# Row sums folded on GpSimd and VectorE instead of TensorE, and float64 weights rebuilt by arithmetic instead of by moved bits, in an attention and feed-forward kernel on one Trainium2 core

## The chip, the cores and the metric

The kernel runs on one core of a Trainium2 chip. The metric is the device time of one execution in microseconds; lower is better. The engines are called PE (TensorE), DVE (VectorE), ACT (ScalarE), POOL (GpSimd) and SP (SyncE, which issues most of the DMAs). Each engine works through its own list of instructions in order, and waits on semaphores for what other engines make.

## The reference

```python
# attention: q, k, v of (8, 12, 448, 64) float32, gains g_q, g_k of 64
q_n, k_n = rmsnorm(q, g_q), rmsnorm(k, g_k)      # x / sqrt(mean(x*x) + 1e-6) * g
attn = softmax(q_n @ k_n.T / sqrt(64))
x = (attn @ v), heads joined                      # (3584, 768)
# feed-forward: w_in (768, 1024) and w_out (1024, 768) are float64, g_ln of 1024
h = x @ w_in
solu = h * softmax(h)
ln = (solu - mean) / sqrt(var + 1e-6) * g_ln
out = (ln @ w_out).astype(float32)                # (3584, 768)
```

The weights come in as float64 numbers, and the kernel makes float32 of them on the chip: it loads each number as two 32-bit words, `lo` and `hi`.

## The kernel before, in words

The function that does the work is `fast_path`. (`general_path`, for inputs outside a range, is behind a branch on a flag that is read at the very end; it does not run here.) Instructions are issued in an order written out by hand: the code runs a list of "units", and after each unit `unit` emits what `later(k, f)` put off for k units, and then one stage of the weight conversion in progress (`feed`).

**Attention.** 48 pairs (8 batches, 6 pairs of heads), index `n`. A pair is loaded four ahead (`load(n + 4)`, eight DMAs of q and k), squared on ACT three ahead (`squares`), and summed along each half row on DVE (`row_sums`, tile `part`, 128 x 28). A row of 64 lies as two halves of 32 in two groups of 32 partitions, so the two half sums must be added across partitions: `fold_sums(n + 2)` does it with a product by a constant matrix `fold` on PE, into a PSUM tile `ss`. From `ss`, `rsqrt_seed` (a logarithm and an exponential on ACT, and `nx` on DVE) and `rsqrt_step` (three small DVE operations) make the reciprocal root `ny`; `normalise` multiplies on POOL (`qkn`), `qk_transpose` transposes on DVE (`qkT`, called T in the prediction), `gain` scales on ACT. Then, for each of four key blocks `kc`: `scores(n, kc)` is two products on PE (`s`) and two exponentials on ACT (`E`); `add` sums the blocks of E for the softmax's denominator, the first on POOL, the other two on DVE (`es`). `values(n - 1)` (`o`) and `sums(n - 1)` (`sm`) on PE stand between the second and the third block of the pair, and `divide(n - 1)` on DVE ends with `xT`.

**PSUM.** The tiles `s`, `ss`, `o`, `sm`, `pu` and `po` share a pool of six buffers (tag "t"); a product waits until an earlier tile's readers have released its buffer. `h` has one buffer of its own.

**Weights.** 12 steps of 512 columns (w_in) during pairs 0 to 11, and 16 steps of 384 columns (w_out) during pairs 12 to 21. A step has four stages: two ACT passes that shift the low word by arithmetic (`low_bits`, lines 469 and 470), two DVE operations on the high word (`high_bits`, 473 and 474), one DVE operation that joins them (`join`, 478), and, for w_out, an ACT pass that multiplies by the gain (`product`, 483). This moving of bits is right only for numbers in a certain range.

**Feed-forward.** 28 tiles of 128 tokens. `ff_in` (`h`) starts in pair 13; `ff_max`, `ff_moments` and `ff_norm` work on DVE, ACT and POOL; `ff_transpose` (`pu`, `uT`) and `ff_out` (`po`, `y`) start in pair 23, when all of w_out is converted. What is left after the last pair is issued unit by unit.

**Check.** During those last units each weight chunk is loaded once more (`again`), `check_w` takes the smallest and largest magnitude of its high words on DVE, and `check_all` puts the result, by a small product on PE (`pw`, line 502), into the flag.

Of the kernel before, what the change touches and what calls it, by code (L numbers as in the profile page):

```python
# [9 lines left out]
FP32 = mybir.dt.float32  # L10
# [356 lines left out]
def fast_path(  # L367
# [7 lines left out]
    out: bass.AP,  # L375
    grow: bass.AP,
    within: bass.AP,
    large: bass.AP,
):


# [24 lines left out]

    ident = consts.tile([P, P], FP32, name="ident")
    ones = consts.tile([P, D], FP32, name="ones")
    fold = consts.tile([P, 2, 2, 32], FP32, name="fold")
    w_in = consts.tile([P, KD, DFF], FP32, name="w_in")  # L410
    w_out = consts.tile([P, KF, DM], FP32, name="w_out")
    gcol = consts.tile([P, KF + 2], FP32, name="gcol")
    mhalf = consts.tile([P, 1], FP32, name="mhalf")
    seven = consts.tile([P, 1], FP32, name="seven")
    eps = consts.tile([P, 1], FP32, name="eps")

    def setup():

        nc.scalar.add_instruction(
            mybir.InstLoadActFuncSet(  # L420
                act_func_set_id=6, name=nc.get_next_instruction_name(), engine=mybir.EngineType.Activation
            )
        )
        nc.gpsimd.memset(mhalf, -0.5)
        nc.gpsimd.memset(seven, 7.0)
        nc.gpsimd.memset(eps, 1e-6)
        nc.gpsimd.memset(ones, 1.0)
        make_identity(nc, ident)

        nc.gpsimd.memset(fold, 0.0)  # L430
        for g in range(4):
            gs = slice(g * 32, g * 32 + 32)
            for x in range(2):
                nc.gpsimd.tensor_copy(fold[gs, g // 2, x], ident[gs, gs])
        pg = ps_t.tile([P, KF + 2], FP32, tag="t", name="pg")
        nc.tensor.transpose(pg, grow, ident[0 : KF + 2, 0 : KF + 2])
        nc.vector.tensor_copy(gcol, pg)

        nc.vector.tensor_scalar(
            gcol[:, KF : KF + 1], gcol[:, KF : KF + 1], gcol[:, KF + 1 : KF + 2], within, OP.mult, OP.mult  # L440
        )

# [13 lines left out]
    def convert_w(step, raw):  # L460

        _, dst, c, cols = step
        n = cols.stop - cols.start
        lo, hi = raw[:, :, 0], raw[:, :, 1]
        tmp = work.tile([P, 2, n], U32, tag="uT", name="tmp")
        t, low = tmp[:, 0], tmp[:, 1].bitcast(FP32)

        def low_bits():
            nc.scalar.activation(low, lo, AF.Relu, scale=-(2.0 ** -29), bias=seven)  # L469
            nc.scalar.activation(tmp[:, 1].bitcast(I32), low, AF.Copy, scale=-1.0, bias=7.0)  # L470

        def high_bits():
            nc.vector.tensor_scalar(t, hi, 3, 0x3FFFFFFF, OP.logical_shift_left, OP.bitwise_and)
            nc.vector.scalar_tensor_tensor(t, hi, 0xC0000000, t, OP.bitwise_and, OP.bitwise_or)  # L474

        def join():
            o = dst[:, c, cols].bitcast(U32) if dst is w_in else t
            nc.vector.tensor_tensor(o, t, tmp[:, 1], OP.bitwise_or)

        def product():  # L480
            if dst is w_out:

                nc.scalar.activation(dst[:, c, cols], t.bitcast(FP32), AF.Copy, scale=gcol[:, c : c + 1])

        return [low_bits, high_bits, join, product]

    def check_w(x, raw):

        hi = raw[:, :, 1].bitcast(FP32)
        nc.vector.tensor_reduce(extent[:, 0, x : x + 1], hi, AX, OP.min, apply_absolute_value=True)  # L490
        nc.vector.tensor_reduce(extent[:, 1, x : x + 1], hi, AX, OP.max, apply_absolute_value=True)

    def check_all():


        worst = small.tile([P, 2], FP32, tag="mv", name="worst")
        one = small.tile([1, 2], FP32, tag="one", name="one")
        pw = ps_t.tile([1, 2, P], FP32, tag="t", name="pw")
        nc.vector.tensor_reduce(worst[:, 0:1], extent[:, 0], AX, OP.min)
        nc.vector.tensor_reduce(worst[:, 1:2], extent[:, 1], AX, OP.max)  # L500
        for i in range(2):
            nc.tensor.transpose(pw[:, i], worst[:, i : i + 1], ident)
        nc.vector.tensor_reduce(one[:, 0:1], pw[:, 0], AX, OP.min)
        nc.vector.tensor_reduce(one[:, 1:2], pw[:, 1], AX, OP.max)
        nc.vector.tensor_scalar(one[:, 0:1], one[:, 0:1], 2.0 ** -15, None, OP.is_ge)
        nc.vector.tensor_scalar(one[:, 1:2], one[:, 1:2], 122880.0, None, OP.is_lt)
        nc.vector.tensor_tensor(one[:, 0:1], one[:, 0:1], one[:, 1:2], OP.mult)

        nc.vector.tensor_scalar(one[:, 1:2], large, -1.0, 1.0, OP.mult, OP.add)
        nc.vector.tensor_tensor(one[:, 0:1], one[:, 0:1], one[:, 1:2], OP.mult)  # L510
        nc.vector.tensor_scalar(large, one[:, 0:1], -1.0, 1.0, OP.mult, OP.add)

    st = {}
    xTs = {}
# [29 lines left out]
    def row_sums(n):  # L544
        d = st[n]
        d["part"] = small.tile([P, 2 * NB], FP32, tag="part", name="part")
        nc.vector.tensor_reduce(d["part"], d["sq"], AX, OP.add)  # L547

    def fold_sums(n):
        d = st[n]  # L550
        d["ss"] = ps_t.tile([P, 2 * NB], FP32, tag="t", name="ss")
        nc.tensor.matmul(d["ss"], fold.rearrange("p h x t -> p (h x t)"), d["part"], start=True, stop=True)

    def rsqrt_seed(n):

# [174 lines left out]
    def unit(f):  # L730
        nonlocal now
        f()
        now += 1
        due = [x for x in todo if x[0] <= now]
        todo[:] = [x for x in todo if x[0] > now]
        for _, g in sorted(due, key=lambda x: x[0]):
            g()
        feed()
# [6 lines left out]
    W_OUT = 22  # L745
    raws = []
    stages = []
    extent = consts.tile([P, 2, len(wq)], FP32, name="extent")
    wdone = 0
    wtarget = 0  # L750

# [34 lines left out]
    def prepare(n):  # L786
        squares(n)
        row_sums(n)

    N = B * NP  # L790
    load(0)
# [7 lines left out]
    with tc.manual_schedule():  # L799
        prepare(0)  # L800
        wtarget = 1
        unit(lambda: fold_sums(0))
        rsqrt_seed(0)
        rsqrt_step(0)
        normalise(0)
        prepare(1)
        qk_transpose(0)
        gain(0)
        unit(lambda: fold_sums(1))
        load(3)  # L810
        rsqrt_seed(1)
        rsqrt_step(1)
# [5 lines left out]
        for n in range(N):  # L818
# [35 lines left out]
                unit(lambda: values(n - 1))  # L854
            if n + 3 < N:
                row_sums(n + 3)
            if n and n + 1 < N:
                load_v(n + 1)
            convert(4)
# [8 lines left out]
        unit(lambda: None)  # L868
        unit(lambda: values(N - 1))
        unit(lambda: sums(N - 1))  # L870

        last = events[at:]
        assert len(last) > len(wq) + 1
        again = [load_w(wq[x]) for x in range(2)]
        for x, (_, f) in enumerate(last):
            unit(f)
            if x < len(wq):
                check_w(x, again[x])
                if x + 2 < len(wq):
                    again.append(load_w(wq[x + 2]))  # L880
            if x == len(wq) + 1:
                check_all()
        for _ in range(4):
            unit(lambda: None)

# [1 line left out]
@with_exitstack  # L887
def kernel(
    ctx: ExitStack,
    tc: tile.TileContext,  # L890
    q: bass.AP,
    k: bass.AP,
    v: bass.AP,
    g_q: bass.AP,
    g_k: bass.AP,
    moe_w_in: bass.AP,
    moe_w_out: bass.AP,
    moe_g_ln: bass.AP,
    out: bass.AP,
):  # L900
    nc = tc.nc
    D = q.shape[3]
    P = 128
    KF = moe_w_in.shape[1] // P
    gains = ctx.enter_context(tc.tile_pool(name="gains", bufs=1))
    grow = gains.tile([KF + 2, P], FP32, name="grow")
    gg = gains.tile([P, 2, D], FP32, name="gg")
    gmax = gains.tile([P, 1], FP32, name="gmax")
    within = gains.tile([P, 1], FP32, name="within")
    flag = gains.tile([1, 1], I32, name="flag")  # L910
    large = gains.tile([1, 1], FP32, name="large")
    nc.scalar.dma_start(grow[0:KF, :], moe_g_ln.rearrange("(c p) -> c p", p=P))
    for i, g in enumerate((g_q, g_k)):
        for h in range(2):
            nc.scalar.dma_start(grow[KF + i : KF + i + 1, h * D : (h + 1) * D], g.rearrange("(o d) -> o d", o=1))
    for i, g in enumerate((g_q, g_k)):
        nc.scalar.dma_start(gg[:, i], g.rearrange("(o d) -> o d", o=1).to_broadcast([P, D]))

    nc.vector.tensor_tensor(gg[:, 0], gg[:, 0], gg[:, 1], OP.mult)
    nc.vector.tensor_reduce(gmax, gg[:, 0], AX, OP.max, apply_absolute_value=True)  # L920
    nc.vector.tensor_scalar(large, gmax[0:1], 80.0 / float(D) ** 0.5, None, OP.is_gt)
    nc.vector.tensor_scalar(within, gmax, 80.0 / float(D) ** 0.5, float(D) ** -0.5, OP.is_le, OP.mult)
    fast_path(tc, q, k, v, moe_w_in, moe_w_out, out, grow, within, large)
    nc.vector.tensor_copy(flag, large)
    other = nc.values_load(flag[0:1, 0:1], min_val=0, max_val=1)
    with tc.If(other > 0):
        general_path(tc, q, k, v, g_q, g_k, moe_w_in, moe_w_out, moe_g_ln, out)


# [28 lines left out]
```

## Time and profile before

| | us |
|---|---|
| median of 4 timed runs | 1127.38 (1127.1 to 1128.03) |
| the profiled execution, its own time | 1126.35 |
| its span in the profile | 1124.5 |
| PE busy | 1041.3 (93%) |
| DVE busy | 604.8 (54%) |
| ACT busy | 381.6 (34%) |
| POOL busy | 210.9 (19%) |

The busy share of an engine is a mean over stages with different limits. By windows of the same trace, PE is busy 625.60 of 625.60 us from 358.70 to 984.30, and 132.11 of 135.70 us from there to 1120; from 55 to 184 us it is busy 100.21 of 129.00 us, DVE 103.93, ACT 64.20 and POOL 41.41. PE's records overlap, so busy PE times of single groups add up to more than they cost. Profile lines show: start and length in us (timeline), or the count, busy time, mean ns of one and the idle time before them with what ended it (groups). In a line, "L552" is line 552 of the kernel before.

### The profile page before, as it was taken

The page shows a single profiled execution, that of the slowest core. Times are in us where ns is not written, and L with a number is a line of the kernel's source. Part 1 is how long each engine was busy: PE and PEld are TensorE (multiplying, and loading weights), DVE is VectorE, ACT ScalarE, POOL GpSimd, SP SyncE. Part 2 cuts the span into 40 slices and gives each one's busy share as a digit, 9 for nine tenths or more (in the row PEclk, how much of TensorE's full clock was granted, in tenths as well). Part 3 has the DMA queues.
Part 4 walks back from the last instruction along what each step waited for, and adds up shares of the span by engine and source line. Part 5 has one row for each costly group of instructions (what it writes and reads, how often), then busy time and mean ns, then how long its engine had stood idle before and what let it go on. Part 6 is the DMA issues. An engine that isn't in the chain of part 4 may idle for free.

```text
span 1124.5 us, 10697 instructions
## 1 busy us (share of the span) xinstructions
PE 1041.3 (93%) x3619; PEld 479.9 (43%) x3619; DVE 604.8 (54%) x1013; ACT 381.6 (34%) x789; POOL 210.9 (19%) x143
## 2 busy tenths in 40 slices
PE   2878788798889999999999999999999999999997
PEld 1323232233334444444444444444444444455554
DVE  3688787455788544444444444444445544555521
ACT  2744554224756222222222222232224322311110
POOL 2432223011333111111111111121111211100000
PEclk9998988999889999999999999999999999999999
DMA  6544334103544111111111111131111201033341
GB/s 129 117 96 98 88 84 98 22 23 67 116 106 75 39 39 39 39 39 38 39 39 33 32 38 39 39 64 30 39 33 33 54 23 59 15 127 117 100 142 42
DMA packets 234426, 70.10 MB, mean 62 GB/s; under 512 B 223600, under 2 KB 223608, under 8 KB 234360
## 3 DMA queue, kind: packets, MB, share of 16 engines
q1 hardware_dynamic: 230016, 58.23, 24.0%
q10 hardware_dynamic: 4344, 11.08, 2.5%
q8 instruction: 31, 0.51, 0.2%
q14 instruction: 35, 0.29, 0.1%
HBM read 58.27 MB, written 11.01 MB: 62 GB/s over the span
## 4 chain that ended last, share of the span: by engine, by line
PE 73%; DVE 13%; ACT 6%; issue 3%; DMA 2%; SPq 2%; POOL 1%; ACTq 0%; DVEq 0%; POOLq 0%
PE h L658 26%; PE po L709 26%; PE s L595 8%; PE o L618 8%; DVE es L609 4%; PE pu L699 2%; PE sm L627 2%; SPq L528 2%; DVE qkT L582 1%; DVE part L547 1%; DVE tmp L474 1%; ACT E L599 1%; ACT qkT L586 1%; DVE r L642 1%; ACT tmp L469 1%
## 5 line engine op out<-in xcount | busy, mean ns | idle before, releaser
L658 PE MATMUL h<-w_in,xT 128*128 128x512 f32 x672 | 308.0, 609 | 11.7 <-DVE u L676 11.7
L709 PE MATMUL po<-w_out,uT 128*128 128x384 f32 x896 | 297.9, 489 | 2.1 <-ACT uT L700 2.1
L709 PEld LDWEIGHTS po<-w_out,uT 128*128 128x128 f32 x896 | 168.3, 190 | 132.0 <-issue 15.0
L595 PE MATMUL s<-qkT 64*112 64x448 f32 x768 | 200.8, 581 | 19.0 <-DVE nx L560 8.4
L599 ACT ACTIVATE E<-s 112x448 f32<-112x448 f32 x384 | 177.3, 546 | 103.9 <-PE s L595 103.8
L658 PEld LDWEIGHTS h<-w_in,xT 128*128 128x128 f32 x672 | 127.3, 194 | 169.4 <-issue 164.7
L618 PE MATMUL o<-E,v 112*64 112x448 f32 x768 | 169.8, 588 | 12.4 <-DVE xT L644 12.4
L607 POOL TENSOR_TENSOR es<-E 112x896 f32<-112x896 f32 x48 | 104.0, 2166 | 325.6 <-ACT E L599 325.6
L595 PEld LDWEIGHTS s<-qkT 64*112 64x112 f32 x768 | 78.2, 176 | 133.7 <-issue 69.0
L609 DVE TENSOR_TENSOR es<-es,E 112x896 f32<-112x896 f32 x96 | 125.0, 1302 | 13.7 <-ACT E L599 10.5
L572 POOL TENSOR_TENSOR qkn<-qk,ny 128x896 f32<-128x896 f32 x48 | 82.8, 1724 | 146.7 <-DVE ny L567 122.8
L700 DVE COPY uT<-pu 128x512 f32<-128x512 f32 x28 | 19.3, 688 | 160.1 <-PE pu L699 144.0
L671 ACT ACTIVATE u<-h,hmax 128x1024 f32<-128x1024 f32 x28 | 31.2, 1115 | 210.6 <-DVE hmax L668 210.6
L710 ACT COPY y<-po 128x384 f32<-128x384 f32 x56 | 26.9, 480 | 213.6 <-PE po L709 213.6
L618 PEld LDWEIGHTS o<-E,v 112*64 112x64 f32 x768 | 54.5, 146 | 102.0 <-issue 83.4
L686 POOL TENSOR_TENSOR he<-he,mhalf 128x1 f32<-128x1 f32 x28 | 21.8, 778 | 382.6 <-DVE he L685 382.6
L668 DVE TENSOR_REDUCE hmax<-h 128x1 f32<-128x1024 f32 x28 | 34.3, 1224 | 80.4 <-PE h L658 80.4
L560 DVE TENSOR_SCALAR nx<-ss 128x28 f32<-128x28 f32 x48 | 9.0, 188 | 115.2 <-ACT ny L559 115.2
L586 ACT ACTIVATE qkT<-qkT,gcol 128x448 f32<-128x448 f32 x48 | 32.6, 680 | 75.6 <-DVE qkT L582 75.6
L640 DVE STREAM_TRANSPOSE r<-sm 128x448 f32<-128x448 f32 x48 | 31.0, 646 | 47.0 <-PE sm L627 47.0
L542 ACT ACTIVATE sq<-qk 128x896 f32<-128x896 f32 x48 | 45.7, 952 | 28.9 <-ACT y L710 11.3
L547 DVE TENSOR_REDUCE part<-sq 128x28 f32<-128x896 f32 x48 | 51.8, 1078 | 6.5 <-ACT sq L542 6.5
(67 smaller groups left out, 610.9 us busy)
## 6 DMA issues: line engine op xcount, KB each, us to landing
raw<-in_moe_w_in_dram SPq DMA_DIRECT2D x24, 512.0 KB, 3.7
raw<-in_moe_w_out_dram SPq DMA_DIRECT2D x32, 384.0 KB, 3.3
qk<-in_q_dram SPq DMA_DIRECT2D x192, 56.0 KB, 2.3
qk<-in_k_dram SPq DMA_DIRECT2D x192, 56.0 KB, 2.3
v<-in_v_dram SPq DMA_DIRECT2D x48, 224.0 KB, 3.0
out_dram<-y ACTq DMA_DIRECT2D x28, 384.0 KB, 2.3
grow<-in_g_q_dram ACTq DMA_DIRECT2D x2, 0.2 KB
grow<-in_g_k_dram ACTq DMA_DIRECT2D x2, 0.2 KB
```

What stands on the lines that cost most here:

```text
L542: nc.scalar.activation(d["sq"], d["qk"].rearrange("p s b d -> p (s b) d"), AF.Square)
L547: nc.vector.tensor_reduce(d["part"], d["sq"], AX, OP.add)
L572: nc.gpsimd.tensor_tensor(d["qkn"], d["qk"].rearrange("p s b d -> p (s b) d"), d["y"].rearrange("p b -> p b ()").to_broadcast([P, 2 * NB, ...
L586: nc.scalar.activation(d["qkT"][:, 0], d["qkT"][:, 0], AF.Copy, scale=gcol[:, KF : KF + 1])
L595: nc.tensor.matmul(s, d["qkT"][hh, 1, kc * SP : (kc + 1) * SP], d["qkT"][hh, 0, :], start=True, stop=True)
L599: nc.scalar.activation(d["E"][:, kc, h], d["s", h], AF.Exp)
L607: nc.gpsimd.tensor_tensor(d["es"], d["E"][:, 0], d["E"][:, 1], OP.add)
L609: nc.vector.tensor_tensor(d["es"], d["es"], d["E"][:, kc], OP.add)
L618: nc.tensor.matmul(d["o"][h * D : (h + 1) * D, :], d["v"][:, h, kc], d["E"][:, kc, h], start=(kc == 0), stop=(kc == NJ - 1),)
L658: nc.tensor.matmul(d["h"][:, hs], xTs[m][:, c, i * P : (i + 1) * P], w_in[:, c, hs], start=(c == 0), stop=(c == KD - 1))
L668: nc.vector.tensor_reduce(nmax, d["h"], AX, OP.max, negate=True)
L709: nc.tensor.matmul(po, d["uT"][:, c], w_out[:, c, hs], start=(c == 0), stop=(c == KF - 1))
```

## The change

Three things change together.

1. *Fold.* `swap_sums` copies the half sums, four groups of 32 partitions, to the neighbouring group on POOL, into an SBUF tile `ss`; it is put off by three units after `row_sums(n + 3)`, so it stands in POOL's list behind the `qkn` of pair n + 2 and before the `es` of pair n + 1, one pair ahead of its use. `fold_sums` then is one DVE addition, between the qkT transpose and `nx`. The `fold` matrix and its product on PE are gone; `ss` no longer takes a PSUM buffer, and `nx` reads SBUF.
2. *Conversion.* Mantissa and exponent are taken apart, made into numbers, and multiplied: `fields` (two DVE operations), `scale` (two ACT passes), `join` (three DVE operations), and `product`, on POOL for w_in and on DVE for w_out. It is right for the whole range of float32.
3. *Check.* The second load of the weights, `check_w` and `check_all` are gone; the flag is written once, at the start.

```diff
-    fold = consts.tile([P, 2, 2, 32], FP32, name="fold")
...
-        t, low = tmp[:, 0], tmp[:, 1].bitcast(FP32)
-        def low_bits():
-            nc.scalar.activation(low, lo, AF.Relu, scale=-(2.0 ** -29), bias=seven)
-            nc.scalar.activation(tmp[:, 1].bitcast(I32), low, AF.Copy, scale=-1.0, bias=7.0)
-        def high_bits():
-            nc.vector.tensor_scalar(t, hi, 3, 0x3FFFFFFF, OP.logical_shift_left, OP.bitwise_and)
-            nc.vector.scalar_tensor_tensor(t, hi, 0xC0000000, t, OP.bitwise_and, OP.bitwise_or)
+        e, m = tmp[:, 0], tmp[:, 1].bitcast(FP32)
+        ei = e.bitcast(I32)
+        def fields():
+            nc.vector.tensor_scalar(tmp[:, 1], hi, 0xFFFFF, None, OP.bitwise_and)
+            nc.vector.tensor_scalar(e, hi, 20, 0x7FF, OP.logical_shift_right, OP.bitwise_and)
+        def scale():
+            nc.scalar.activation(m, tmp[:, 1], AF.Copy, scale=2.0 ** -20, bias=1.0)
+            nc.scalar.activation(ei, ei, AF.Relu, bias=m896)
         def join():
-            o = dst[:, c, cols].bitcast(U32) if dst is w_in else t
-            nc.vector.tensor_tensor(o, t, tmp[:, 1], OP.bitwise_or)
+            nc.vector.scalar_tensor_tensor(m, lo, 2.0 ** -52, m, OP.mult, OP.add)
+            nc.vector.tensor_scalar(ei, ei, 255.0, 2.0 ** 23, OP.min, OP.mult)
+            nc.vector.scalar_tensor_tensor(e, hi, 0x80000000, e, OP.bitwise_and, OP.bitwise_or)
         def product():
-            if dst is w_out:
-                nc.scalar.activation(dst[:, c, cols], t.bitcast(FP32), AF.Copy, scale=gcol[:, c : c + 1])
+            if dst is w_in:
+                nc.gpsimd.tensor_tensor(dst[:, c, cols], m, e.bitcast(FP32), OP.mult)
+            else:
+                nc.vector.scalar_tensor_tensor(
+                    dst[:, c, cols], m, gcol[:, c : c + 1], e.bitcast(FP32), OP.mult, OP.mult
+                )
...
+    def swap_sums(n):
+        d = st[n]
+        d["ss"] = small.tile([P, 2 * NB], FP32, tag="ss", name="ss")
+        for g in range(4):
+            o = g ^ 1
+            nc.gpsimd.tensor_copy(d["ss"][g * 32 : g * 32 + 32], d["part"][o * 32 : o * 32 + 32])
     def fold_sums(n):
         d = st[n]
-        d["ss"] = ps_t.tile([P, 2 * NB], FP32, tag="t", name="ss")
-        nc.tensor.matmul(d["ss"], fold.rearrange("p h x t -> p (h x t)"), d["part"], start=True, stop=True)
+        nc.vector.tensor_tensor(d["ss"], d["ss"], d["part"], OP.add)
...
     def prepare(n):
         squares(n)
         row_sums(n)
+        swap_sums(n)
...
             if n + 3 < N:
                 row_sums(n + 3)
+                later(3, lambda n=n: swap_sums(n + 3))
...
-        again = [load_w(wq[x]) for x in range(2)]
-        for x, (_, f) in enumerate(last):
+        for _, f in events[at:]:
             unit(f)
-            if x < len(wq):
-                check_w(x, again[x])
-                if x + 2 < len(wq):
-                    again.append(load_w(wq[x + 2]))
-            if x == len(wq) + 1:
-                check_all()
```

More of the change, by code (lines that the diff above doesn't have):

```diff
@@ L377, in fast_path @@
     within: bass.AP,
-    large: bass.AP,
 ):
@@ L413, in fast_path @@
     mhalf = consts.tile([P, 1], FP32, name="mhalf")
-    seven = consts.tile([P, 1], FP32, name="seven")
+    m896 = consts.tile([P, 1], FP32, name="m896")
     eps = consts.tile([P, 1], FP32, name="eps")
@@ L424, in setup @@
         nc.gpsimd.memset(mhalf, -0.5)
-        nc.gpsimd.memset(seven, 7.0)
+        nc.gpsimd.memset(m896, -896.0)
         nc.gpsimd.memset(eps, 1e-6)
@@ L428, in setup @@
         make_identity(nc, ident)
[L430 to L434, printed above, removed]
         pg = ps_t.tile([P, KF + 2], FP32, tag="t", name="pg")
@@ L480, in product @@
         def product():
-            if dst is w_out:
-                nc.scalar.activation(dst[:, c, cols], t.bitcast(FP32), AF.Copy, scale=gcol[:, c : c + 1])
[L485 to L511, printed above, removed]
@@ L513, in fast_path @@
+            if dst is w_in:
[4 more added lines that the diff above has]
+                )
+        return [fields, scale, join, product]
     st = {}
@@ L747, in fast_path @@
     stages = []
-    extent = consts.tile([P, 2, len(wq)], FP32, name="extent")
     wdone = 0
@@ L801, in fast_path @@
         wtarget = 1
-        unit(lambda: fold_sums(0))
+        fold_sums(0)
         rsqrt_seed(0)
@@ L808, in fast_path @@
         gain(0)
-        unit(lambda: fold_sums(1))
+        fold_sums(1)
+        unit(lambda: None)
         load(3)
@@ L870, in fast_path @@
         unit(lambda: sums(N - 1))
-        last = events[at:]
-        assert len(last) > len(wq) + 1
-        again = [load_w(wq[x]) for x in range(2)]
-        for x, (_, f) in enumerate(last):
+        for _, f in events[at:]:
             unit(f)
-            if x < len(wq):
-                check_w(x, again[x])
-                if x + 2 < len(wq):
-                    again.append(load_w(wq[x + 2]))
-            if x == len(wq) + 1:
-                check_all()
         for _ in range(4):
@@ L910 @@
     flag = gains.tile([1, 1], I32, name="flag")
-    large = gains.tile([1, 1], FP32, name="large")
     nc.scalar.dma_start(grow[0:KF, :], moe_g_ln.rearrange("(c p) -> c p", p=P))
@@ L920 @@
     nc.vector.tensor_reduce(gmax, gg[:, 0], AX, OP.max, apply_absolute_value=True)
-    nc.vector.tensor_scalar(large, gmax[0:1], 80.0 / float(D) ** 0.5, None, OP.is_gt)
+    nc.vector.tensor_scalar(flag, gmax[0:1], 80.0 / float(D) ** 0.5, None, OP.is_gt)
     nc.vector.tensor_scalar(within, gmax, 80.0 / float(D) ** 0.5, float(D) ** -0.5, OP.is_le, OP.mult)
[L923 to L926, printed above, removed]
+    fast_path(tc, q, k, v, moe_w_in, moe_w_out, out, grow, within)
+    large = nc.values_load(flag[0:1, 0:1], min_val=0, max_val=1)
+    with tc.If(large > 0):
         general_path(tc, q, k, v, g_q, g_k, moe_w_in, moe_w_out, moe_g_ln, out)
```

## The prediction

> **What bounds the kernel now.** First the page's slices: where is TensorE (PE) full, and where is it not?
>
> ```profile
> PE   2878788798889999999999999999999999999997
> DVE  3688787455788544444444444444445544555521
> PEclk9998988999889999999999999999999999999999
> ```
>
> Each digit is 28.1 us. From slice 14 on PE is full; asked by windows, it is busy 625.60 of the 625.60 us from 358.7 to 984.3. Before 358.7 us it is not, and VectorE (DVE) is at 7 to 8 tenths. So the span has two regimes: 358.7 us of attention pairs with the weight conversion beside them, and 766 us in which only PE time counts. Next, the groups that the change touches:
>
> ```profile
> L552 PE MATMUL ss<-part,fold 128*128 128x28 f32 x96 | 21.0, 300 | 21.3 <-DVE part L547 14.5 <-DVE r L640 3.8 <-ACT E L599 3.0
> L560 DVE TENSOR_SCALAR nx<-ss 128x28 f32<-128x28 f32 x48 | 9.0, 188 | 115.2 <-ACT ny L559 115.2
> L609 DVE TENSOR_TENSOR es<-es,E 112x896 f32<-112x896 f32 x96 | 125.0, 1302 | 13.7 <-ACT E L599 10.5
> ```
>
> Columns: busy us, mean ns, idle before and its releaser. Seen: DVE stands 115.2 us at L560 behind ScalarE (ACT), and 1302 ns is a mean over adds of 1.08 us and stretched ones. The timeline of one w_in pair shows both; pairs repeat every 12.88 us (qkT transpose T at 123.81 and 136.70):
>
> ```profile
> 132.17 2.46 POOL L607 TENSOR_TENSOR es<-E 112x896 f32<-112x896 f32 x1 [0.43 <-ACT E L599]
> 132.61 4.18 DVE L609 TENSOR_TENSOR es<-es,E 112x896 f32<-112x896 f32 x2
> 136.70 1.10 DVE L582 STREAM_TRANSPOSE qkT<-qkn 128x896 f32<-128x896 f32 x1
> 137.84 0.67 ACT L586 ACTIVATE qkT<-qkT,gcol 128x448 f32<-128x448 f32 x1 [5.74 <-DVE qkT L582]
> 138.41 0.75 ACT L469 ACTIVATE tmp<-raw,seven 128x512 f32<-128x512 uint32 x1
> 139.19 0.63 ACT L470 ACTIVATE tmp<-tmp 128x512 int32<-128x512 f32 x1
> 139.73 0.27 ACT L559 ACTIVATE ny<-ss,eps 128x28 f32<-128x28 f32 x1
> 140.03 0.19 DVE L560 TENSOR_SCALAR nx<-ss 128x28 f32<-128x28 f32 x1 [2.22 <-ACT ny L559]
> ```
>
> The loop is DVE's: T, then through ACT (gain, both low-bit passes, the logarithm) back to nx, 2.22 us idle; the rest of DVE's list; then two adds of 4.18 us instead of 2.2, because GpSimd (POOL) is in its own add. That last point prices the change, so here is its clearest pair of rows:
>
> ```profile
> 326.06 2.08 POOL L607 TENSOR_TENSOR es<-E 112x896 f32<-112x896 f32 x1 [2.76 <-ACT E L599]
> 326.15 2.40 DVE L474 SCALAR_TENSOR_TENSOR tmp<-raw,tmp 128x384 uint32<-128x384 uint32 x1
> ```
>
> L474 of 384 columns takes 0.56 us elsewhere; here it ends 0.41 us after POOL does. T, `part`, and the divide's transposes keep their times under POOL. I call this the lock: a DVE operation on two SBUF tensors and a POOL operation exclude each other.
>
> **The change, part by part.** Times are of the profiled execution (1126.35 us, span 1124.5); the median of the four timed runs, 1127.38, is 1.03 above it, which I add at the end. About 0.2%, 2.25 us, is what a measurement can tell from no change.
>
> 1. *PE fold, full stage.* Around a fold PE's rows start at
>
> ```profile
> 444.38 1.76 PE L595 MATMUL s<-qkT 64*112 64x448 f32 x8
> 446.07 0.41 PE L552 MATMUL ss<-part,fold 128*128 128x28 f32 x2
> 446.32 1.07 PE L699 MATMUL pu<-ident,u 128*128 128x128 f32 x8
> ```
>
> so a fold costs 0.25 us, not its 0.60 busy. 44 of the 96 records lie after 358.7: 22 x 0.25 = **-5.5**. Its substitutes there (four copies of about 0.2 us by L434's 204 ns, one addition of 0.19 by L566) lie under full PE with DVE 48% busy: nothing. The copies are made a pair ahead, so the addition waits for nothing.
>
> 2. *Check and second weight load.* 28 x 1.21 us of DVE and 28 loads lie under PE. On the path is only the last tile: pw waits 1.02 us for L500, and that tile's transposes-to-product distance is 2.28 us (1106.80 to 1109.08) against 1.73 (1082.44 to 1084.17): **-0.5**. The flag was ready at 1110.8, 14 us before the end: moving it is nothing.
>
> 3. *Pairs with w_in (n = 2 to 11).* New DVE list: T, two field operations, addition, nx, `part`, three small, divide (four), three join operations, two adds. nx reads SBUF and no longer stands behind ACT; ACT does the logarithm before the scale passes. New POOL list: qkn, product, four copies, add. Walk, from T's start (512-column prices: L473 0.42, L474 0.69): copies end at 0.85, POOL's add holds the lock 0.9 to 3.0 (2.09); the field operations wait for it and end at 3.6; addition 3.7, nx 3.9, `part` 4.9, three small 5.4, divide 7.6 (as now 2.25), join 8.2, 8.5, 9.25; first add to 10.25; POOL's product, queued since 9.4, takes the lock to 11.45; second add 12.4; next T at 12.3. Lock time 3.0 us. The product shows nowhere: by columns it is 0.97 (qkn 1.70 x 512/896) to 1.20 (add 2.09 x 512/896), and 2.09 at worst; I take 1.2. 10 x (12.3 - 12.88) = **-5.8**; between 11.3 (copies and fields free of the lock) and 13.2 per pair it is -16 to +3.
>
> Whether the single-input field operations wait is thinly shown: L690, also a TENSOR_SCALAR, took 1.93 us under qkn at 246.54 against 0.81; L473 itself only brushes POOL (0.42 for 0.35 at 294.03). I take it that they wait, by L690's row. If they did not, only the addition would, and the pair would be 11.7, the term -11.8. The Trainium skill, "SBUF — State Buffer", section Who interferes with whom, says that a tensor_scalar from SBUF to SBUF can run in a two-port mode and then blocks and is blocked for the whole GpSimd instruction, as a two-input operation is. That rule speaks against the change, as it gives the -5.8 and not the -11.8; L690's row agrees with it.
>
> 4. *Start.* qkn(1) now stands behind pair 2's copies in POOL's queue, and qkn(2) behind the first product; it needs ny, waits out add and joins on DVE (as its 3.02 us at 35.41 does now), and ends near 41.0 instead of 38.4; T follows, +3.2. Pair 1 then has POOL's add, product and copies in one pair: 10.0 instead of 8.0 us. **+5.2**; 0 if the copies slip between, +7 if each race is lost.
>
> 5. *Into and through the feed-forward pairs (n = 12 to 15).* The fold at 185.89 waited 1.63 us for a score buffer before h could start at 186.34; the last scores before it end at 184.26: -2.1. Two folds at 0.25: -0.5. At n = 15 nx stood until 271.90 behind ACT; by the same list the next T comes at 279.4 for 280.63: -1.2. **-3.8**; -1 if the next buffer waits in the fold's stead.
>
> 6. *Pairs with w_out (n = 16 to 21, 280.63 to 351.16), ten steps.* Busy DVE time per step: now 0.35 + 0.56 + 0.56; then two fields, joins 0.56, 0.35, 0.56 and a product 0.56: +1.26, less three overlaps of 0.1: ten steps +9.6. Addition: 6 x 0.2 = +1.2. DVE's waits for ACT in these pairs (0.97, 2.35, 1.42, 2.22, 2.50, 0.97, and 1.63 + 0.55 at adds) go: -12.6; new ones come, joins behind the scale passes twice 0.9 and the second add twice 0.8: +3.4. Lock: now 3.3 (1.84 at 326.15, 1.15 at 318.24, 0.3 small); DVE's list becomes dense, so nearly all of POOL's 2.09 falls on locked work: 6 x 1.9 = 11.4, +8.1. **+9.7**; +1.5 with the lock as now, +18 if copies and qkn are met too.
>
> Sum: -5.5 - 0.5 - 5.8 + 5.2 - 3.8 + 9.7 = -0.7, 1125.65 on the profile's scale, 1126.7 on the median's.
>
> **Rivals.** *A, DVE gets the lock first.* The second add directly follows the first, and at 35.41 POOL did lose to back-to-back DVE work (3.02 us for 1.70). Then a w_in pair is 11.8 (-5.0 more) and the w_out lock halves (-4): 1117.7, 1116 to 1121. Against it: the second add depends on the first, and at 119.3 POOL won before an add. *B, slower: the lock becomes the bound.* Place: n = 2 to 21, where POOL now has product and copies and DVE more two-input work. If the product costs as the whole add, 2.09, and POOL wins each race, a w_in pair has 3.9 us of lock and lasts 13.2: 10 x 0.9 = +9, 1136. It decides above 3.3 us of lock per w_in pair, with w_out as summed. For it: POOL shared nothing with DVE but two operations per pair so far; against: the product has 512 columns, not 896. *C, the change doesn't do what it says on PE*: ten tiles of the six score buffers instead of eleven fall on other banks, a new wait takes the fold's 0.25 us, and term 1 is 0: 1132. Against: from 358.7 on PE waits for DVE nowhere, with 5 us of h between a divide and the next scores.
>
> **Numbers.** Forecast 0.42 (1126.7; own range 1122 to 1131, a third of it under 1125.1 and about a quarter over 1129.6), A 0.27, B 0.24, C 0.07. Faster: 0.14 + 0.27 = 0.41; slower: 0.11 + 0.24 + 0.07 = 0.42; same 0.17. Both signs hold most of the chance, so the range reaches over A and B: 1116 to 1138.
>
> **What would show it.** Right: no L552 rows and PE distance 1.69 from scores to pu; nx without an ACT wait; w_in pairs of 12.3 with two stretched places (fields, second add); w_out pairs about 1.6 us longer; T of pair 2 near 41.7. Wrong: w_in pairs under 12 (A) or over 13 with a product near 2 us (B); gaps on PE after its full stage starts (C); a start as now, which would make the sum -6.

## The result, and the profile after

The changed kernel takes 1128.85 us (median of 41 runs, 1124.75 to 1131.28), the kernel before 1127.2 (62 runs, 1125.34 to 1128.84): a ratio of 1.0012, 95% interval 1.0008 to 1.0017. It is slower by 1.65 us. That is under the 0.2% that the prediction set as its bound, but outside the uncertainty, and on the other side of the forecast, which was 0.7 us faster. The execution profiled first, 1124.68 us (span 1122.9), is shorter than all 41 timed ones; experiments 7 and 8 give two more profiles of the same program.

First the slices of the profile's page.

```profile
PE   1777869798878999999999999999999999999997
DVE  3899999567999444555555544454446644522300
PEclk9788888899888999999999999999999999999999
```

DVE is now at 8 or 9 tenths in slices 1 to 6, where it was at 6 to 8, and PE's granted clock is lower there: by windows 0.85 from 60 to 160 us, where the kernel before had 0.94. Next the groups that replace those of before (busy us, mean ns, idle before).

```profile
L538 DVE TENSOR_SCALAR nx<-ss 128x28 f32<-128x28 f32 x48 | 28.8, 599 | 1.2
L530 DVE TENSOR_TENSOR ss<-ss,part 128x28 f32<-128x28 f32 x48 | 23.5, 489 | 1.2 <-POOL ss L526 1.1
L587 DVE TENSOR_TENSOR es<-es,E 112x896 f32<-112x896 f32 x96 | 115.1, 1199 | 15.1 <-ACT E L577 12.1
```

There is no product for the fold. `nx` has lost its 115.2 us behind ACT. It and the addition show means of 599 and 489 ns, for 180 where nothing blocks them: blocked time counts as busy. Of the 28.8 us of `nx`, 21.8 lie in the full stage, where DVE does not set the pace. In the w_in pairs other operations are blocked, as the timeline of one shows (T at 137.45, the next at 149.77):

```profile
134.36 3.16 DVE L587 TENSOR_TENSOR es<-es,E 112x896 f32<-112x896 f32 x2
134.53 2.06 POOL L474 TENSOR_TENSOR w_in<-tmp 128x512 f32<-128x512 f32 x1 [2.14 <-DVE tmp L470]
136.65 1.67 POOL L526 COPY ss<-part 32x28 f32<-32x28 f32 x4
137.45 1.10 DVE L560 STREAM_TRANSPOSE qkT<-qkn 128x896 f32<-128x896 f32 x1
138.40 2.08 POOL L585 TENSOR_TENSOR es<-E 112x896 f32<-112x896 f32 x1
138.48 2.28 DVE L460 TENSOR_SCALAR tmp<-raw 128x512 uint32<-128x512 uint32 x1
140.68 0.42 DVE L461 TENSOR_SCALAR tmp<-raw 128x512 uint32<-128x512 uint32 x1
141.02 0.18 DVE L530 TENSOR_TENSOR ss<-ss,part 128x28 f32<-128x28 f32 x1
```

The two stretched places are the ones that the prediction named: POOL's product stands between the two adds (3.16 for 2.2), and POOL's add, 138.40 to 140.48, shuts out the first field operation, which ends 0.28 behind it. DVE has no idle left in this pair; it lasts 12.32 us. The field operation has a single input, and it is shut out all the same: 2.28 us for 0.42. The Trainium skill, "SBUF — State Buffer", section Who interferes with whom, says that a tensor_scalar can enter a two-port mode and then contends with GpSimd, where the instruction that issues second is blocked; this row agrees.

In the full stage the same place as before reads

```profile
446.23 1.76 PE L573 MATMUL s<-qkT 64*112 64x448 f32 x8
447.93 1.09 PE L677 MATMUL pu<-ident,u 128*128 128x128 f32 x8
```

1.70 from scores to `pu`, where it was 1.94.

The next table gives the stages, from the start times of T. T of pairs 13, 17, 23 and 25 bound them, in order: start and w_in; feed-forward entry; w_out; entry to the full stage; full stage and tail. All are lengths in us, and a row's sum is the span.

| kernel | to T13 | T13-T17 | T17-T23 | T23-T25 | T25-end |
|---|---|---|---|---|---|
| before | 175.34 | 105.29 | 70.53 | 26.21 | 747.13 |
| changed, first profile | 174.41 | 99.49 | 77.13 | 28.70 | 743.17 |
| changed, second profile | 173.97 | 98.74 | 77.09 | 32.21 | 743.09 |
| changed, third profile (experiment 7) | 174.76 | 99.45 | 77.01 | 32.98 | 742.96 |
| fold alone | 148.28 | 99.19 | 64.40 | 32.31 | 743.42 |
| conversion alone | 159.87 | 97.24 | 78.34 | 26.33 | 747.52 |
| copies early | 166.14 | 96.77 | 77.43 | 31.95 | 742.81 |
| one addition behind uT | 174.44 | 99.03 | 77.03 | 30.31 | 743.29 |
| before, passes later | 147.96 | 100.02 | 63.74 | 26.48 | 747.40 |
| passes later and fold | 148.54 | 99.62 | 63.94 | 30.84 | 743.36 |

### The profile page after: what moved, and what is told of

Its sections match the earlier page's. It is cut to its first block, busy times and chain, and to the rows that moved or that the text cites. A ratio compares the mean times of both kernels' runs of the same rounds, so it can differ in the third digit from the quotient of the medians.

```text
span 1122.9 us, 10684 instructions
## 1 busy us (share of the span) xinstructions
PE 1022.5 (91%) x3521; PEld 461.6 (41%) x3521; DVE 642.2 (57%) x1066; ACT 373.8 (33%) x773; POOL 293.9 (26%) x338
## 4 chain that ended last, share of the span: by engine, by line
PE 71%; DVE 18%; issue 5%; ACT 2%; SPq 2%; DMA 1%; POOL 0%; ACTq 0%; DVEq 0%; POOLq 0%
PE po L687 26%; PE h L636 25%; PE s L573 8%; PE o L596 7%; DVE es L587 3%; DVE tmp L460 2%; PE pu L677 2%; DVE qkT L560 2%; SPq L498 2%; PE sm L605 2%; DVE r L620 1%; DVE tmp L468 1%; DVE ss L530 1%; DVE r L618 1%; DVE xT L622 1%
## 5 line engine op out<-in xcount | busy, mean ns | idle before, releaser
L573 PE MATMUL s<-qkT 64*112 64x448 f32 x768 | 198.0, 606 | 66.0 <-DVE r L618 26.7
L573 PEld LDWEIGHTS s<-qkT 64*112 64x112 f32 x768 | 73.8, 183 | 178.8 <-ACT E L577 73.7
L587 DVE TENSOR_TENSOR es<-es,E 112x896 f32<-112x896 f32 x96 | 115.1, 1199 | 15.1 <-ACT E L577 12.1
L526 POOL COPY ss<-part 32x28 f32<-32x28 f32 x192 | 63.6, 331 | 26.0 <-DVE part L517 17.2
L560 DVE STREAM_TRANSPOSE qkT<-qkn 128x896 f32<-128x896 f32 x48 | 52.9, 1103 | 2.4 <-POOL qkn L550 2.4
L654 DVE TENSOR_TENSOR u<-h,u 128x1024 f32<-128x1024 f32 x28 | 34.3, 1224 | 33.6 <-ACT u L649 33.6
```

Source lines behind the costliest of these rows:

```text
L526: nc.gpsimd.tensor_copy(d["ss"][g * 32 : g * 32 + 32], d["part"][o * 32 : o * 32 + 32])
L560: nc.vector.transpose(d["qkT"].rearrange("p s t -> p (s t)"), d["qkn"].rearrange("p b d -> p (b d)"))
L573: nc.tensor.matmul(s, d["qkT"][hh, 1, kc * SP : (kc + 1) * SP], d["qkT"][hh, 0, :], start=True, stop=True)
L587: nc.vector.tensor_tensor(d["es"], d["es"], d["E"][:, kc], OP.add)
```

## The experiments

Ratios are against runs of the kernel before on the same chip (medians 1126.6 to 1127.13).

**1. The fold alone.** The kernel before with `swap_sums` and the DVE addition; conversion and check kept.

```diff
+                later(3, lambda n=n: swap_sums(n + 3))
-        nc.tensor.matmul(d["ss"], fold.rearrange("p h x t -> p (h x t)"), d["part"], start=True, stop=True)
+        nc.vector.tensor_tensor(d["ss"], d["ss"], d["part"], OP.add)
```

> The row-sum fold of the change alone (GpSimd copies, VectorE addition); the weight conversion by bits and the check stay as before. Theory 1, two opposite parts: the fold is the gaining half. In a w_in pair nx no longer stands 2.22 us behind ScalarE, and the addition and its lock cost 0.2 to 1: pairs of 12.88 become 11.0 to 11.8, ten of them -11 to -19; start +2 to +6; full stage 21 folds at 0.17 = -3.6; so 1104 to 1117 us. Theory 2, the lock sets the w_in pair whatever is folded: pairs stay near 12.3 to 12.9, only the full stage gains, 1118 to 1125. Theory 3, the copies themselves are the cost of the change: slower than before, 1128 or more.

Measured: 1089.98 us (1089.44 to 1092.94), ratio 0.968 (0.9667 to 0.9692): 37 us faster, more than any theory allowed. W_in pairs are 10.07 us instead of 12.88. POOL's add now starts behind the copies, when T has begun, so DVE's two `es` adds take 2.29 us undisturbed, and only the addition is caught (1.34). Here are the copies and the adds of one pair; POOL's add of the next starts at 108.22, 0.22 us after T:

```profile
104.94 3.21 POOL L548 COPY ss<-part 32x28 f32<-32x28 f32 x4
105.79 2.29 DVE L609 TENSOR_TENSOR es<-es,E 112x896 f32<-112x896 f32 x2
```

**2. The conversion alone.** The changed kernel with the fold put back on PE.

```diff
-                later(3, lambda n=n: swap_sums(n + 3))
-        nc.vector.tensor_tensor(d["ss"], d["ss"], d["part"], OP.add)
+        nc.tensor.matmul(d["ss"], fold.rearrange("p h x t -> p (h x t)"), d["part"], start=True, stop=True)
```

> The other half alone: conversion by arithmetic and no check, the fold as the small TensorE product of before. Theory 1 (opposite parts): nx is again behind ScalarE's scale passes and the fields and joins add VectorE work and lock, so w_in pairs of 13.5 to 14.5 (+6 to +16) and w_out pairs 1 to 2 us longer (+6 to +12): 1138 to 1155 us. Theory 2 (lock alone sets the pair): w_in pairs near 13, 1130 to 1138. Theory 3 (copies are the cost): about as before or faster, 1122 to 1128.

Measured: 1113.21 us (1111.06 to 1113.28), ratio 0.9876 (0.9862 to 0.9891): 14 us faster. All three theories missed. The two halves gain 37 and 14 us alone and lose 1.65 together. The w_in pair is 11.11 us; in these pairs `nx` does not wait for ACT, although the fold is on PE (later in the kernel it does, up to 5.60 us): in this kernel's order ACT's two passes come after the logarithm. So each half takes away the same 2.22 us of idle time.

**3. No range check.** The check and the second load are left out of the kernel before.

```diff
-                check_w(x, again[x])
...
-                check_all()
```

> The kernel before without the range check of the weights and without their second load (the check is left out, nothing else). By the prediction's term 2: -0.5 us, 1126.7. Rival, the 28 loads and 28 pairs of reductions in the last 140 us cost PE more than the last tile's 0.55: 1122 to 1125.

Measured: 1126.29 us, ratio 0.9994 (0.9985 to 1.0003): not told apart from nothing, and compatible with -0.5; the rival's 1122 to 1125 did not come. At the place named, the last tile's transposes to product, the distance is 1.78 us instead of 2.28.

**4. W_in product on VectorE.**

```diff
-                nc.gpsimd.tensor_tensor(dst[:, c, cols], m, e.bitcast(FP32), OP.mult)
+                nc.vector.tensor_tensor(dst[:, c, cols], m, e.bitcast(FP32), OP.mult)
```

> The changed kernel with the w_in product on VectorE instead of GpSimd. If GpSimd's product holds the lock against the second add (theory: the add shows about 2.1 for 1.08), VectorE pays 0.69 by its 512-column two-input row and saves about 1.0 per w_in pair, and GpSimd's queue at the start is shorter: 1122 to 1127 us. If the product costs the pair nothing, VectorE's 0.69 is simply added: ten pairs +7, 1134 to 1137.

Measured: 1121.22 us (1116.6 to 1122.0), ratio 0.9934 (0.9917 to 0.995), the gain a little over what was expected. DVE pays 0.68 us for the product, the field operations are free (0.38 and 0.41), POOL's add instead meets the second add (2.97), and the pair is 11.84.

**5 and 6. The copies two units earlier**, in the changed kernel and in the fold alone.

```diff
-                later(3, lambda n=n: swap_sums(n + 3))
+                later(1, lambda n=n: swap_sums(n + 3))
```

> The changed kernel with the four copies issued two units earlier, so that GpSimd's order in a pair is add, copies, qkn, product instead of add, qkn, product, copies. Theory (place of GpSimd's add): with the copies ahead of it, the add starts only when T ends and shuts out the field operations for 1.9 us (126.06 to 128.15 in the profile); without them it starts 1.7 earlier, T covers half of it, the fields wait 0.2 to 0.9 as in the run with the conversion alone (1.28 for 0.4), and a w_in pair lasts 11.1 to 11.5 instead of 12.32: ten pairs -8 to -12, 1116 to 1121 us. Rival 1, the lock time is the same wherever it falls: pairs stay at 12.3, 1127 to 1130. Rival 2, the copies now stand in front of qkn and T waits for it: pairs of 12.7, 1131 to 1134.

> The fold alone (conversion by bits and check as before) with the same earlier copies; a candidate to beat both kernels. Theory (place of GpSimd's add): in the fold-alone run the add, behind the copies, made the addition wait 1.17 us; free of them it moves up beneath T and the pair loses about 1 us: 9.0 to 9.6 instead of 10.07, nine pairs, 1080 to 1086 us. Rival, the add moves onto VectorE's second add instead, which then takes 2.1 for 1.1 as in the kernel before: pairs of 10.0 to 10.6, 1089 to 1095.

Measured: the changed kernel 1117.68 us, ratio 0.9927 (0.9915 to 0.994), w_in pairs of 11.44, as the theory said. The fold alone 1098.94, ratio 0.9753 (0.974 to 0.9765), which is 9 us worse than in experiment 1: pairs of 10.92. That is the rival's place, and a larger loss than it allowed (pairs of 10.6, 1095 us). The same edit helps one kernel and hurts the other, by where it puts POOL's add. In the changed kernel (the first two lines) it moves half beneath T; in the fold alone (the last two) it lands on the adds:

```profile
120.36 1.10 DVE L560 STREAM_TRANSPOSE qkT<-qkn 128x896 f32<-128x896 f32 x1
121.39 1.28 DVE L460 TENSOR_SCALAR tmp<-raw 128x512 uint32<-128x512 uint32 x1
```

```profile
131.76 4.02 DVE L609 TENSOR_TENSOR es<-es,E 112x896 f32<-112x896 f32 x2
132.75 2.08 POOL L607 TENSOR_TENSOR es<-E 112x896 f32<-112x896 f32 x1 [1.70 <-ACT E L599]
```

**7. An eleventh score tile.** One allocation per pair that nothing writes.

```diff
+        d["bank"] = ps_t.tile([P, 2 * NB], FP32, tag="t", name="bank")
```

> The changed kernel with one more score-bank allocation per pair that nothing writes, so that the six buffers rotate as they did with the product's tile. If the 1.57 us that PE's o waits for VectorE's uT at 359.4, and its second scores' waits for r, come from the shorter rotation (the prediction's C at one place), the entry to the full stage is 1.6 to 2.5 us earlier: 1125 to 1127.5 us. If the rotation does not matter, or the allocation itself makes somebody wait as the product did, 1128 to 1130.

Measured: 1127.6 us (1125.67 to 1129.36), ratio 1.0006 (0.9997 to 1.0015). It does not test the rotation. The tile that nothing writes changes no buffer: the built program has the changed kernel's instructions and buffers, one by one. So this is a repeat of the changed kernel, on the chip of experiment 8, and shows that two medians of one program can lie 1.2 us apart (1127.6 and 1128.77). Its profiled execution took 1128.98 us, and PE's `o` idles 4.01 us for `uT` at the entry.

**8. The changed kernel again.**

> The changed kernel once more, unaltered, for a second profiled execution: the first (1124.68) lies 4.2 us under the median of 41 runs. Theory: the spread of its runs is made before 360 us, where GpSimd and VectorE race for the lock, so that T of pair 24 differs by 1 to 5 us between the two executions while the stretch from T of pair 25 to the end (743 us) is equal within 0.3. Rival: the granted clock varies, and the difference lies in the full stage.

Measured: 1128.77 us (1126.4 to 1131.0, 12 runs), ratio 1.0019 (1.0011 to 1.0028). Its profiled execution took 1126.89, 2.2 us more than the first. The stages show one place where it is longer: T23-T25, 32.21 instead of 28.70. The theory was right that the full stage is equal (743.17 and 743.09), but not in what T of pair 24 tells: it differs by 1.23 us, and it is the slower execution that has it earlier. The loss comes right behind it. Here is that place, in the second profile:

```profile
356.92 1.09 PE L677 MATMUL pu<-ident,u 128*128 128x128 f32 x8
357.90 1.10 DVE L560 STREAM_TRANSPOSE qkT<-qkn 128x896 f32<-128x896 f32 x1
358.77 2.08 POOL L585 TENSOR_TENSOR es<-E 112x896 f32<-112x896 f32 x1 [0.47 <-ACT E L577]
358.93 1.96 DVE L530 TENSOR_TENSOR ss<-ss,part 128x28 f32<-128x28 f32 x1
360.81 0.68 DVE L678 COPY uT<-pu 128x512 f32<-128x512 f32 x1
361.54 4.92 PE L596 MATMUL o<-E,v 112*64 112x448 f32 x16 [3.53 <-DVE uT L678]
```

The addition stands on DVE in front of the `uT` copy. POOL's add is 0.16 us ahead of it here, so it takes 1.96 us, `uT` is late, and PE, which from here on should be full, is idle for 3.53 us. `o` does not read `uT`; it waits for the copy because the program gave it the buffer of `pu`'s second half, as the buffer numbers in the built program show. In the first profile the two start within 0.02 us, and the addition passes; `nx`, behind the copy, is held up in its place:

```profile
360.14 2.11 POOL L585 TENSOR_TENSOR es<-E 112x896 f32<-112x896 f32 x1 [0.62 <-ACT E L577]
360.16 0.15 DVE L530 TENSOR_TENSOR ss<-ss,part 128x28 f32<-128x28 f32 x1
360.83 1.47 DVE L538 TENSOR_SCALAR nx<-ss 128x28 f32<-128x28 f32 x1
360.96 3.23 PE L596 MATMUL o<-E,v 112*64 112x448 f32 x16 [1.57 <-DVE uT L678]
```

And in the kernel before, with the product, `o` had another buffer, which an exponential on ACT had released, and did not wait at all:

```profile
357.64 1.09 PE L699 MATMUL pu<-ident,u 128*128 128x128 f32 x8 [0.52 <-DVE xT L644]
358.67 3.23 PE L618 MATMUL o<-E,v 112*64 112x448 f32 x16
```

`o` itself takes 4.92 us after the long idle and 3.23 after the short one. The windows of the second profile (PE busy first, granted clock third from last) show why:

```profile
358.00:361.50 3.50, 0.01 (x1) 0.00 (x0) 3.50 (x4) 2.31 (x6) 2.33 (x3) 1.00 0.70 128
361.50:366.50 5.00, 4.96 (x18) 1.76 (x20) 1.64 (x5) 0.00 (x0) 2.50 (x5) 0.66 0.23 42
```

The clock is 0.66 over the five microseconds after the idle. So the lost race costs 1.96 us of idle and 1.69 of slow products, 3.65 together; T24 to T25 differs by 3.51 between the two profiles (24.11 and 20.60).

**9. One addition behind uT**, in the changed kernel.

```diff
+                if n == W_OUT + 1:
+                    later(1, lambda n=n: fold_sums(n + 2))
+                else:
+                    fold_sums(n + 2)
```

> The changed kernel with one of its 48 additions moved: at n = 23 the addition is issued one unit later, behind VectorE's uT copy, which PE's o waits for because it was given the buffer of that copy's source. Theory (one race at the entry to the full stage makes both the loss and the spread): the addition no longer stands 1.3 to 2.0 us in front of the copy, PE's idle before o falls from 3.5 to about 1.6 us, o takes 3.23 instead of 4.92 us, T of pair 24 to T of pair 25 lasts 20.6 as in the luckier first profile: 1128.8 - 3.5 = 1125 to 1126 us, with less spread. Rival: the loss there is PE work that is only queued up, whatever DVE does: 1128 to 1129, T to T still 24.

Measured: 1124.68 us (1123.71 to 1127.89, 11 runs), ratio 0.998 (0.9971 to 0.9989), apart from the unaltered kernel's intervals (1.0011 to 1.0028 in experiment 8, 0.9997 to 1.0015 in 7): one moved addition of 48 turns the change from slower to faster. The profile bears the theory out in part only:

```profile
360.21 1.01 DVE L530 TENSOR_TENSOR ss<-ss,part 128x28 f32<-128x28 f32 x1
360.34 4.92 PE L596 MATMUL o<-E,v 112*64 112x448 f32 x16 [2.78 <-DVE uT L678]
```

The addition is behind the copy now, but PE's idle before `o` is 2.78 us (expected 1.6): the transposes of `pu` had ended at 357.6, and T, which also stands in front of `uT`, ended only at 359.7; `o` still takes 4.92, and T23-T25 is 30.31, which is 4.1 more than before the change. So the addition is a part of the loss; the rest is the wait for the copy itself and the slow products behind it.

**10. The same one addition in the fold alone.** The diff is that of experiment 9.

> The fold alone (conversion by bits and check of before) with the same one addition behind the uT copy; a candidate to beat all. In the fold-alone run the addition took 1.57 us there, PE idled 4.65 us and o took 4.92. Theory: 1.5 of idle and up to 1.7 of o go: 1086.5 to 1088.5 us. Rival, PE is idle there for T and the es adds, not for the addition: 1089.5 to 1090.5.

Measured: 1088.18 us (1083.74 to 1089.67), ratio 0.9646 (0.9628 to 0.9665), against 0.968 (0.9667 to 0.9692) without it. PE idles 1.39 us before `o` instead of 4.65, and `o` takes 3.23, as the theory said.

**11. Passes later.** Two stages of the kernel before exchanged, nothing else.

```diff
-        return [low_bits, high_bits, join, product]
+        return [high_bits, low_bits, join, product]
```

> The kernel before with two conversion steps exchanged: VectorE's two bit operations first, ScalarE's two low-bit passes one unit later, so that the logarithm no longer stands behind them; fold, check and arithmetic as before. Theory (each half of the change removes the same wait, which is why their gains do not add): nx loses its 2.22 us idle, the bit operations stand right behind T in reach of GpSimd's add (up to 0.9 of wait): w_in pairs of 10.6 to 11.6 instead of 12.88, 1108 to 1118 us without either half. Rival: the pair is held by the lock or by ACT's whole list and the wait only moves: 1125 to 1130.

Measured: 1088.0 us (1086.77 to 1088.33), ratio 0.9649 (0.9636 to 0.9662). This one line gains 39 us, without either half of the change. W_in pairs alternate between 8.65 and 11.27, 9.96 on average, and pairs and time are below what was expected (10.6 and 1108 at the least): in every second pair POOL's add falls beneath T, and DVE's adds take 1.08 and 1.09; in the others it meets the second one, which takes 2.79. From the timeline of one pair:

```profile
121.09 0.26 ACT L559 ACTIVATE ny<-ss,eps 128x28 f32<-128x28 f32 x1
121.43 0.18 DVE L560 TENSOR_SCALAR nx<-ss 128x28 f32<-128x28 f32 x1
121.52 0.74 ACT L469 ACTIVATE tmp<-raw,seven 128x512 f32<-128x512 uint32 x1
```

The logarithm is in front of the passes, and in these pairs `nx` follows the bit operations without a wait (in the kernel before it stood idle 2.22 us).

**12. Passes later and the fold**, with the one addition behind `uT`.

> The kernel before with the exchanged conversion steps of the run before last, the GpSimd/VectorE fold, and the one addition behind uT; conversion arithmetic and check as before. If the two gains were independent, -39 and -37 us would add to about 1050. Theory (both remove the same wait, so only the rest of each adds): w_in pairs stay at 9.8 to 10.0, the full stage loses 3.7 us as with every fold, and o's wait for uT at its entry costs 2 to 4 us against the run without the fold: 1083 to 1088 us. Rival, the added VectorE and GpSimd work costs more than is left to gain: 1089 to 1095.

Measured: 1087.97 us (1085.46 to 1088.35), ratio 0.965 (0.9637 to 0.9664). Nothing is added: the full stage gains 4.0 us by the fold (743.36 for 747.40), and the entry gives 4.4 of it back (30.84 for 26.48). Experiments 10, 11 and 12 are the best versions, 39 us under the kernel before and 41 under the changed one, and not told apart.

## Why the prediction was wrong

**W_in pairs and start (terms 3 and 4): right.** Predicted 12.3 us per pair with the lock at the fields and at the second add; 12.32, at those two places. Predicted -0.6 to T of pair 13; -0.93 and -1.37 in the two profiles. T of pair 2 was put at 41.7 and came at 40.70 and 41.20; T of pair 3 was put 5.2 later and came 6.6 and 5.2 later. In the first profile these are two errors that cancel in part: the start lost 6.6 where 5.2 was put, and the pairs behind it gained 7.5 where 5.8 was put. Of POOL's recorded 2.05 us for the product some 0.9 is waiting, until the first add has ended; where it ran by itself, near 43.7 us, it took 1.26, near the 1.2 that was taken.

**Feed-forward entry (term 5): direction right, size short.** -3.8 was predicted; -5.8 and -6.6 came. In the first profile `h` starts 7.75 us after T of pair 13 instead of 11.00, a gain of 3.2 where 2.1 was put, and the last pair gains the 1.2 that was put; the other 1.4, for 0.5 put for two folds, was not traced.

**W_out (term 6): right in kind, too large.** +9.7 was predicted, +6.6 came in both profiles. DVE's waits for ACT, 12.6 us, went as walked; of the 3.4 us of new waits only 1.3 is found in either profile, so 2.1 of the 3.1 us too many lie there.

**Entry to the full stage: the step that failed.** The sum has no term for it. Term 6 ends at DVE's T, term 1 puts the substitutes of the fold "under full PE with DVE 48% busy: nothing", and rival C is set aside because "from 358.7 on PE waits for DVE nowhere". All three take it that PE starts full as before. In its place the runs show a new wait of PE for DVE: `o` has got the buffer of `pu`'s second half, and waits for the `uT` copy. Where 0 had been taken, the entry grew by 2.5, 6.0 and 6.8 us in the three profiles of the changed program. The 2.5 came although the addition was not blocked there (0.15 us); in the other two it was blocked (1.96 and 1.32) in front of the copy, and the products behind the idle time were slow as well.

That the wait comes with the fold is shown: in all ten profiles with the fold on DVE, `o` has the buffer of `pu` in the built program and waits for `uT`, 1.39 to 4.91 us; in all four with the product on PE, the conversion alone among them, it has another, waits for nothing, and the entry is 26.2 to 26.5 us. Experiment 9 shows what the addition adds: with it moved, the median is 1124.68. A kernel with the fold on DVE and another buffer for `o` was not run. The prediction held this mechanism in rival C, other buffers and a new wait, but looked for it in each of the 22 pairs; it costs most where PE goes full, once.

Without the entry the three profiles are 4.2, 5.5 and 4.1 us faster than before, not 0.7. That the total missed by so little is luck: the other terms were too high by 3.4 to 4.8 us, and the missing one was of the same size.

**Full stage and tail (terms 1 and 2): too large.** -4.0 for -6.0. A fold is worth 0.22 us (29.55 to 29.33 us from T to T of most pairs), not 0.25, and one pair near 875 us gained a wait of 0.52 for a score buffer. Behind T of pair 47, where the check's gain must lie, 0.3 to 0.4 us are gained for 0.5.

**From profile to median.** The first profile agrees with the sum by luck: -1.67 for -0.7, because it won the race. The step of +1.03 assumed that the changed kernel stands to its median as the one before does; it stands 4.2 us under it. The second profile is +0.54 against the profile before, the third +2.63; the median's +1.65 lies between them. The race was lost in two of these three executions; how often it is lost in those that were not profiled is not known.

**The rivals.** A (DVE wins the lock, pairs of 11.8) and B (pairs of 13.2) did not happen; C did, at one place. What neither the forecast nor a rival saw is that the two halves are not additive: the wait that each removes is one and the same, and it was ACT's order, not the amount of work, that made it (experiment 11). Some 41 of the 53 us that are missing from the sum of the two gains lie before T of pair 13, and why is seen in the w_in pairs: the conversion alone 11.11, the addition 0.2 more, and POOL's add, pushed from T onto the fields by the copies, 1.0 more, is 12.3. Experiment 5, which takes only that push away, has 11.44.

## What to carry to other kernels

When an engine's list is full of short operations, ask for each new one what stands behind it in that list and who waits for that; moving one 0.15 us operation, which was blocked for up to 2 us in front of a copy, turned the sign here. A tile taken out of a shared pool changes which buffers later tiles get, and so what they wait for: look at the place where the busiest engine goes full. Two edits that remove the same wait do not add, so price a change against each of its halves; and before replacing work, try reordering it, since exchanging two stages was worth 39 us here. Where two engines exclude each other, as POOL and DVE do in these traces, look at the place of the blocking operation and not only at its length: the part of POOL's add that lay beneath T held up nothing, since T took its 1.10 us all the same (experiments 1 and 5).

## What was not expected of the hardware

How PE's speed depends on the length of an idle stretch: at the entry, after 1.39 and 1.57 us of idle time `o` took 3.23 us; in six profiles with 2.68 to 4.65 us it took 4.92, with a granted clock of 0.66 in the first 5 us. The length alone does not decide it: after 4.01 us (experiment 7) `o` took 6.24 us, with a clock of 0.50, and after 4.91 us (experiment 6) 5.42. The Trainium skill, "TensorE: Matmul & The Clock Gate", section What's actually happening, has half clock after an idle window of about 3.4 us, and a busy window as long until full clock returns. The 1.69 us lost fit the second part (half speed for about 3.4 us); for the first, 2.68 us of recorded idle (experiment 12) was enough here.

A group of four copies on POOL, 0.92 us by itself, took up to 3.21 us where DVE's two-input operations stood close together, in the fold alone; there POOL's next add came behind DVE's adds instead of onto them, and that kernel is 9 us faster than the one with early copies (experiments 1 and 6).
